# Q of two pieces moved from SyncE's queue to GpSimd's, a first GEMM in two column halves, earlier scaling of V, and a last quarter copied by two engines

## The chip, the cores and the metric

The kernel runs on 1 core of a Trainium2 chip (trn2). The metric is the time of one execution on the device in microseconds; the median of several runs is compared.

## The reference

The kernel computes a retention layer followed by a feed-forward block. There are 8 batches, 8 heads, 576 positions and a head size of 64; the feed-forward block has a width of 512 and an inner width of 2048.

```python
scores = scale * np.matmul(q, k.transpose(0, 1, 3, 2))
Dmat = np.where(rel >= 0, gamma[:, None, None] ** rel[None, :, :], 0.0)
x = np.matmul(scores * Dmat[None], v)          # (B, H, S, D)
x = x.transpose(0, 2, 1, 3).reshape(B * S, H * D)
h = x @ w_in
out = (h * np.clip(h + 3.0, 0.0, 6.0) / 6.0) @ w_out   # (4608, 512)
```

## The kernel before

The sequence of each batch is cut into four pieces of 128 positions and a rest of 64; the rests of two batches make one piece. There are 36 pieces, numbered c. For each piece Q, K and V are brought in for all heads ("thirds" of a piece, 128 rows of 8 x 64 numbers). The decay is folded into factors per position: Q and V are scaled, a mask leaves the lower triangle, and a state (K times V) is carried from piece to piece. `scale_v(c)` scales V on VectorE (L245), `k_by_pe` transposes K on TensorE and copies the result with ScalarE (L256, L257), `q_by_pe` does the same for Q through a product with a diagonal matrix (L265, L272), `scores` multiplies them and masks on VectorE (L347), `state_early` (L314 to L323) updates the state of pieces 0 to 3, `inter` and `intra` add up the piece's output (L361, L372), which ScalarE copies into `xt`, the transposed input of the first GEMM.

Tokens go through the feed-forward block in 9 blocks `kb` of 512 columns (four pieces each, the last block the rests). The first GEMM makes 16 row groups `fc` of 128 (`g1`, matmuls at L577, or `g1_columns` at L600 for a part of the columns), followed by an activation on ScalarE (L585) and a product on VectorE (L586). The second GEMM of blocks 0 and 1 goes over `w_out` directly (L635); from block 2 on it is made of seven products of half size (`g2_seven`, L720), whose results are added or copied and stored by quarter. In the last block the last quarter is copied in two halves by `copy_half` (L751), each followed by its own stores (L625); the other quarters are stored by `store_quarter` (L688), one half by SyncE's (SP's) queue and one by ScalarE's.

The order of instructions on each engine is the order in which the program is written (a manual schedule); each engine takes its own in order and waits on semaphores. The functions `first_step`, `step_first` and `step_second` place the work of later pieces between the units of the GEMMs.

Transfers: GpSimd's queue brings K and V (and Q from piece 4 on) and the weights, with a cast from float32 to float16 on the way (L103, L131, L136). Q of pieces 0 to 3 comes by SP's queue as float32 (`load_q`, L120), those of 2 and 3 held until a matmul of piece 0 has been issued, and is cast by ScalarE (`cast_q`, L128). The first GEMM of block 0 begins with `g1_first`: the first two row groups over all 512 columns, in two halves of the inner dimension.

Of the kernel before, what the change touches and what calls it, by code (L numbers as in the profile page):

```python
# [17 lines left out]
def kernel(  # L18
# [16 lines left out]
    nc = tc.nc  # L35
# [3 lines left out]
    P = 128  # L39
# [4 lines left out]
    MBLK = 512  # L44
# [48 lines left out]
    NBUF = 11  # L93

    def load_third(c, i):
        if i == 0:
            kn = nat.tile([P, H, D], FP16, tag="kn", bufs=NBUF, name=f"kn_{c}")
            qv = nat.tile([P, 2, H, D], FP16, tag="qv", bufs=NBUF, name=f"qv_{c}")
            loaded[c] = {"kn": kn, "qv": qv, "q16": qv[:, 0], "dma": []}
        dst, src = ((loaded[c]["kn"], k), (loaded[c]["qv"][:, 0], q),  # L100
                    (loaded[c]["qv"][:, 1], v))[i]
        for p0, b, s0, n in pieces[c][3]:
            loaded[c]["dma"].append(nc.gpsimd.dma_start(  # L103
                dst[p0:p0 + n], src[b, :, s0:s0 + n, :].rearrange("h s d -> s h d")))

    def load(c):
        for i in range(3):
            load_third(c, i)

    def load_kv(c):  # L110
        load_third(c, 0)
        load_third(c, 2)

    plain_q = {}

    def load_q(c, after=None):
        qf = work.tile([P, H, D], FP32, tag="osb", bufs=4, name=f"qf_{c}")
        plain_q[c] = qf
        (p0, b, s0, n), = pieces[c][3]
        moved = nc.sync.dma_start(qf, q[b, :, s0:s0 + n, :].rearrange("h s d -> s h d"))  # L120
        if after is not None:
            tc.add_manual_dep(
                moved.ins, after.ins.name,
                mybir.DependencyInfo(mybir.DependencyClass.Sync, mybir.DependencyReason.DATA),
                reason="the first pieces have the queues")

    def cast_q(c):
        nc.scalar.copy(loaded[c]["q16"], plain_q[c])  # L128
# [16 lines left out]
    load_q(0)  # L145
    load_q(1)
    load_kv(0)
    zeros = const.tile([P, MBLK], FP16)
    nc.vector.memset(zeros, 0.0)
    cb = const.tile([P, 2], FP32)  # L150
# [446 lines left out]
    def g1_columns(kb, fc, ph, cols):  # L597

        for dmc in range(NCC):
            nc.tensor.matmul(ph[:, cols], win16[:, dmc, P * fc:P * fc + P],  # L600
                             xt_of(kb)[:, dmc, cols],
                             start=(cols.start == 0 and dmc == 0),
                             stop=(cols.stop == MBLK and dmc == NCC - 1),
                             skip_group_check=True)
        if cols.stop == MBLK:
            g1_act(kb, ph, fc)

    def g1_first(kb):

        banks = [g1_bank(kb, fc) for fc in range(2)]  # L610
        for dmcs in ((0, 1), (2, 3)):
            for fc in range(2):
                g1_mm(kb, banks[fc], fc, dmcs)
        for fc in range(2):
            g1_act(kb, banks[fc], fc)

    def store(kb, mc, cols, src):
        if kb < B:
# [59 lines left out]
    def store_quarter(kb, i, j, src):  # L678

        cols = slice(NH * j, NH * j + NH)  # L680
        if kb < B:
            r0 = kb * S + TH * i
            nc.sync.dma_start(out[r0:r0 + TH, cols].rearrange("(u p) n -> p u n", u=2), src)
        else:
            rest = out.rearrange("(m x s) n -> x s m n", x=2, s=S)
            for x in range(2):
                queue = nc.scalar if x else nc.sync
                queue.dma_start(rest[x, MAIN:S, 2 * i:2 * i + 2, cols],  # L688
                                src[x * HALF:x * HALF + HALF])

    def g2_seven(kb, last=False):

        gt = gts[kb]

        def w(i, j):
            return wout16[:, KH * i:KH * i + KH, NH * j:NH * j + NH]

        def a(i, j):
            return gt[:, KH * j:KH * j + KH, TH * i:TH * i + TH]

        def s(name):
            return sums[kb, name]

        acc = {}

        def get(name):
            if name not in acc:
                if last and name == "x":
                    acc[name] = [psum.tile([P, NH], FP32, tag=t, name=f"x{t}_{kb}")
                                 for t in ("o", "tu")]  # L710
                else:
                    whole = bank([P, 2, NH], FP32, name=f"{name}_{kb}")
                    acc[name] = [whole[:, 0], whole[:, 1]]
                    wholes[name] = whole
            return acc[name]

        def product(name, u, left, right, first):
            dst = get(name)[u]
            for c in range(KH):
                newest[0] = nc.tensor.matmul(  # L720
                    dst, left()[:, c, P * u:P * u + P], right[:, c, :],
                    start=(first and c == 0 and (u == 0 or name not in wholes)),
                    stop=(c == KH - 1), skip_group_check=True)

        kept, wholes = {}, {}

        def parts(name, tile):
            if name in wholes:
                return [(wholes[name], tile)]
            return [(acc[name][u], tile[:, u]) for u in range(2)]  # L730

        def keep(name):
            kept[name] = work.tile([P, 2, NH], FP32, tag="keep_" + {"m5": "m1"}.get(name, name), bufs=1,
                                   name=f"keep_{name}_{kb}")
            for src, dst in parts({"m5": "z"}.get(name, "x"), kept[name]):
                nc.scalar.copy(dst, src)

        def total(i, j, name, src):
            osb = work.tile([P, 2, NH], FP32, tag="osb", bufs=4, name=f"osb_{kb}_{i}_{j}")
            for (a0, dst), (_, a1) in zip(parts(src, osb), parts(src, kept[name])):  # L740
                nc.vector.tensor_tensor(out=dst, in0=a0, in1=a1, op=ALU.add)
            store_quarter(kb, i, j, osb)

        def copy_total():
            osb = work.tile([P, 2, NH], FP32, tag="osb", bufs=4, name=f"osb_{kb}_1_0")
            nc.scalar.copy(osb, wholes["x"])
            store_quarter(kb, 1, 0, osb)

        def copy_half(u):
            osb = work.tile([P, NH], FP32, tag="osb", bufs=4, name=f"osh_{kb}_{u}")  # L750
            nc.scalar.copy(osb, acc["x"][u])  # L751
            store(kb, 2 + u, slice(0, NH), osb)

        def unit(name, u, left, right, first, then=()):
            def do():
                product(name, u, left, right, first)
                for f in then:
                    f()
            return do

        plan = [
            ("x", lambda: a(0, 0), w(0, 0), True, [lambda: keep("m1")]),
            ("y", lambda: a(0, 1), w(1, 0), True,
             [lambda: total(0, 0, "m1", "y"), lambda: token_sums(kb, "s3")]),
            ("x", lambda: s("s2"), wts["t2"], False, [lambda: keep("u2")]),
            ("z", lambda: s("s1"), wts["t1"], True,
             [lambda: keep("m5"), lambda: token_sums(kb, "s4")]),
            ("x", lambda: s("s3"), wts["t3"], False, [lambda: total(1, 1, "m5", "x")]),
            ("z", lambda: s("s4"), w(1, 1), False, [lambda: total(0, 1, "u2", "z")]),
            ("x", lambda: a(1, 1), wts["t4"], False, [] if last else [copy_total]),  # L770
        ]
        units = []
        for n, (name, left, right, first, then) in enumerate(plan):
            for u in range(2):
                after = then if u else []
                if last and n == len(plan) - 1:
                    after = [lambda u=u: copy_half(u)]
                units.append(unit(name, u, left, right, first, after))
        return units
# [1 line left out]


    WQ = DFF // 4
    for c in range(1, EARLY):
        load_kv(c)
    load_win(0, WQ // 2)
    load_win(WQ // 2, WQ)
    for i in range(1, 4):
# [5 lines left out]

    scale_v(0)
    q_by_pe(0)
    load_q(2, newest[0])
    warm(2, MBLK)
    cast_q(1)
    k_by_pe(0)  # L800
    load_q(3, newest[0])
    fill_gfull()
    for c in range(EARLY):
        if c:
# [2 lines left out]
        if c < EARLY - 1:  # L807
            scores(c)
            run_later(9)
            if c:  # L810
                k_by_pe(c + 1)
            state_early(c)
            run_later(9)
            if not c:
                k_by_pe(c + 1)
            q_by_pe(c + 1)
            if c + 2 < EARLY:
                cast_q(c + 2)
            scale_v(c + 1)
        else:  # L820
            scores_last(c)
# [40 lines left out]
    def first_step(c):  # L862


        old, new, b = c - 1 >= EARLY, c + 1 < 8, pieces[c - 1][1]
        if old:
            before = state_of.get(b)
            o = bank_or(None if c == 6 else "o", [P, NPAIR, P], FP32, name=f"o_{c - 1}")
# [20 lines left out]
            copy()  # L889
        if c < 8:  # L890
            run_later(9)
        if EARLY <= c < 8:
            scale_v(c)

    def transpose_q_and_load(c):

# [205 lines left out]
```

## Time and profile before

| | us |
|---|---|
| median of 3 runs | 294.66 (294.29 to 294.87) |
| the profiled execution, its own time | 294.43 |
| its span in the profile | 292.6 |
| TensorE busy | 281.1 |
| VectorE busy | 227.6 |
| ScalarE busy | 169.1 |
| GpSimd busy | 104.3 |

The granted TensorE clock was 1.0 of full speed throughout. In a line of the timeline the first number is the start, the second the time taken, both in us from the start of the span; then follow the engine (PE is TensorE, PEld its weight load, DVE VectorE, ACT ScalarE, POOL GpSimd, SP SyncE; a q behind the name is the engine's queue of transfers), the line of the kernel, the operation with its output and inputs, and in brackets the idle time of the engine before it and what ended that. A line of the chain of waits has a start, a duration and what took it. A line of the windows has the stretch, its length and the busy time of TensorE, its weight loads, VectorE, ScalarE and GpSimd. A line of the issues of transfers has the size and the median time from the issue to the landing.

### The profile page before, as it was taken

The page shows a single profiled execution, that of the slowest core. Times are in us where ns is not written, and L with a number is a line of the kernel's source. Part 1 is how long each engine was busy: PE and PEld are TensorE (multiplying, and loading weights), DVE is VectorE, ACT ScalarE, POOL GpSimd, SP SyncE. Part 2 cuts the span into 40 slices and gives each one's busy share as a digit, 9 for nine tenths or more (in the row PEclk, how much of TensorE's full clock was granted, in tenths as well). Part 3 has the DMA queues.
Part 4 walks back from the last instruction along what each step waited for, and adds up shares of the span by engine and source line. Part 5 has one row for each costly group of instructions (what it writes and reads, how often), then busy time and mean ns, then how long its engine had stood idle before and what let it go on. Part 6 is the DMA issues. An engine that isn't in the chain of part 4 may idle for free.

```text
span 292.6 us, 8351 instructions
## 1 busy us (share of the span) xinstructions
PE 281.1 (96%) x3492; PEld 174.7 (60%) x3492; DVE 227.6 (78%) x377; ACT 169.1 (58%) x301; POOL 104.3 (36%) x130
## 2 busy tenths in 40 slices
PE   7699999999989999999999999999999999999993
PEld 2454445544544587458745874587458745874682
DVE  4858656798758997899789988998899588728860
ACT  6668537784357744774486448644864286338711
POOL 8753578159523432443234324455550000000000
PEclk9999999999999999999999999999999999999999
DMA  9999999999999989997999799979992240120014
GB/s 137 177 205 203 191 157 215 165 126 137 132 215 166 160 85 120 168 141 81 121 163 143 77 127 170 136 82 123 160 139 47 74 110 0 38 81 30 0 39 109
DMA packets 156631, 36.21 MB, mean 124 GB/s; under 512 B 143792, under 2 KB 155568, under 8 KB 156592
## 3 DMA queue, kind: packets, MB, share of 16 engines
q0 software_dynamic: 113104, 17.83, 89.3%
q1 hardware_dynamic: 42896, 17.31, 30.5%
q8 instruction: 27, 0.44, 0.7%
q10 hardware_dynamic: 592, 0.52, 0.5%
q14 instruction: 12, 0.10, 0.1%
HBM read 36.70 MB, written 9.44 MB: 158 GB/s over the span
## 4 chain that ended last, share of the span: by engine, by line
PE 91%; DMA 4%; POOL 2%; DVE 1%; issue 1%; ACT 0%; ACTq 0%; POOLq 0%
PE ph L577 41%; PE x L720 14%; PE pout L635 9%; PE z L720 8%; PE y L720 5%; DMA kn<-in_k_dram 3%; PE o L483 3%; PE sc L450 2%; PE o L504 1%; PE u L535 1%; PE ph L600 1%; POOL kn L103 1%; DMA out_dram<-osb 1%; PE xtu L720 1%; PE xo L720 1%
## 5 line engine op out<-in xcount | busy, mean ns | idle before, releaser
L577 PE MATMUL ph<-xt,win 128*128 128x512 f16 x560 | 122.3, 379 | 0.0
L586 DVE SCALAR_TENSOR_TENSOR gt<-u,ph 128x512 f16<-128x512 f32 x144 | 95.7, 685 | 22.6 <-ACT u L585 21.4
L585 ACT ACTIVATE u<-ph,cb 128x512 f32<-128x512 f32 x144 | 98.4, 688 | 25.7 <-PE ph L577 25.1
L577 PEld LDWEIGHTS <-win 128*128 128x128 f16 x560 | 54.7, 98 | 64.4
L103 POOL DMA_DIRECT2D kn<-in_k_dram x40 | 34.0, 850 | 40.7 <-PE ph L577 15.4
L103 POOL DMA_DIRECT2D qv<-in_v_dram x40 | 33.8, 846 | 38.8 <-PE ph L577 16.2
L720 PEld LDWEIGHTS <-sum_s 128*128 128x128 f16 x448 | 42.7, 98 | 5.3
L103 POOL DMA_DIRECT2D qv<-in_q_dram x36 | 30.2, 839 | 28.7 <-PE z L720 10.4
L720 PEld LDWEIGHTS <-gt 128*128 128x128 f16 x336 | 32.1, 98 | 5.5
L635 PE MATMUL pout<-wout,gt 128*128 128x512 f16 x128 | 29.6, 379 | 0.1
L720 PE MATMUL x<-wsum_t,sum_s 128*128 128x256 f16 x192 | 22.9, 273 | 0.0
L556 ACT CAST tm<-th 128x256 f16<-128x256 f32 x24 | 9.7, 405 | 20.3 <-DVE th L551 20.1
L635 PEld LDWEIGHTS <-gt 128*128 128x128 f16 x128 | 11.9, 98 | 13.2 <-issue 0.4
L456 DVE TENSOR_TENSOR at<-sc,mask 128x1024 f16<-128x1024 f32 x14 | 17.0, 1217 | 1.9 <-PE sc L450 1.9
L676 DVE TENSOR_TENSOR sum_s<-gt 128x1024 f16<-128x1024 f16 (+1 forms) x21 | 18.1, 864 | 0.2
L332 DVE TENSOR_TENSOR qv<-qv,gqv 128x1024 f16<-128x1024 f16 x26 | 17.8, 684 | 0.0
L514 ACT CAST xt<-o 128x512 f16<-128x512 f32 x28 | 15.0, 585 | 4.6 <-PE o L504 4.6
L567 DVE TENSOR_TENSOR ta<-u,th 128x256 f32<-128x256 f32 x24 | 10.2, 424 | 6.3 <-ACT th L554 5.2
L720 PE MATMUL z<-wout,sum_s 128*128 128x256 f16 x112 | 14.5, 274 | 0.0
L720 PE MATMUL y<-wout,gt 128*128 128x256 f16 x112 | 14.3, 273 | 0.0
L720 PE MATMUL z<-wsum_t,sum_s 128*128 128x256 f16 x112 | 13.6, 273 | 0.0
L720 PE MATMUL x<-wout,gt 128*128 128x256 f16 x96 | 11.5, 272 | 0.0
(118 smaller groups left out, 255.3 us busy)
## 6 DMA issues: line engine op xcount, KB each, us to landing
out_dram<-osb SPq DMA_DIRECT2D x32, 256.0 KB, 3.2
kn<-in_k_dram POOLq DMA_DIRECT2D x32, 128.0 KB, 5.9
qv<-in_v_dram POOLq DMA_DIRECT2D x32, 128.0 KB, 6.0
qv<-in_q_dram POOLq DMA_DIRECT2D x28, 128.0 KB, 5.9
wout<-in_moe_w_out_dram POOLq DMA_DIRECT2D x4, 512.0 KB, 15.2
win<-in_moe_w_in_dram POOLq DMA_DIRECT2D x3, 512.0 KB, 12.3
qf<-in_q_dram SPq DMA_DIRECT2D x4, 256.0 KB, 4.6
win<-in_moe_w_in_dram POOLq DMA_DIRECT2D x2, 256.0 KB, 8.3
```

Of the source, the lines that this page charges most:

```text
L103: loaded[c]["dma"].append(nc.gpsimd.dma_start(dst[p0:p0 + n], src[b, :, s0:s0 + n, :].rearrange("h s d -> s h d")))
L332: scaled = nc.vector.tensor_tensor(out=qv, in0=qv, in1=gqv, op=ALU.mult)
L456: nc.vector.tensor_tensor(out=at.rearrange("t a j p s -> t (a j p) s"), in0=sc.rearrange("t a j p s -> t (a j p) s"), in1=mask64[:, None, ...
L514: nc.scalar.copy(xt_at(cs[0], 0, 2 * P).rearrange("e p (j x s) -> e p j x s", j=2, x=2) [:, :, :, half, :], o[half].rearrange("e j p s -> ...
L556: nc.scalar.copy(tm, ta)
L567: nc.vector.tensor_tensor(out=ta, in0=st[c]["u"][1], in1=st[c]["sum"], op=ALU.add)
L577: newest[0] = nc.tensor.matmul(ph, win16[:, dmc, P * fc:P * fc + P], xt_of(kb)[:, dmc, :], start=(dmc == 0), stop=(dmc == NCC - 1))
L585: nc.scalar.activation(u, ph, ACTF.Relu, bias=cb[:, 0:1], scale=1.0 / 6.0)
L586: nc.vector.scalar_tensor_tensor(out=gts[kb][:, fc, :], in0=u, scalar=1.0, in1=ph, op0=ALU.min, op1=ALU.mult)
L635: nc.tensor.matmul(pout, gt[:, fc, P * mc:P * mc + P], wout16[:, fc, :], start=(fc == 0), stop=(fc == NFC - 1))
L676: nc.vector.tensor_tensor(out=s(which)[:, c0:c1], in0=x(), in1=y(), op=op)
L720: newest[0] = nc.tensor.matmul(dst, left()[:, c, P * u:P * u + P], right[:, c, :], start=(first and c == 0 and (u == 0 or name not in whol ...
```

## The change

Six edits. (1) `load_q` is used for pieces 0 and 1 only; Q of pieces 2 and 3 comes by GpSimd's queue, already cast, ahead of K and V of the same piece (`load_qkv`); K and V of piece 1 keep their place behind those of piece 0. (2) In the loop over the first pieces Q's product comes ahead of K's transposition for every piece, and both after the state product. (3) `g1_first` makes the first two row groups in two halves of 256 columns each, over the whole inner dimension. (4) `first_step` scales V of pieces 4 to 7 at its beginning and not at its end. (5) In the last block, one half of the quarter of the first rows and second columns is stored by GpSimd's queue in place of ScalarE's. (6) In the last block, the second half of the last quarter is copied by VectorE in place of ScalarE.

```diff
--- before.py
+++ after.py
@@ -93,7 +93,7 @@
     NBUF = 11
 
     def load_third(c, i):
-        if i == 0:
+        if c not in loaded:
             kn = nat.tile([P, H, D], FP16, tag="kn", bufs=NBUF, name=f"kn_{c}")
             qv = nat.tile([P, 2, H, D], FP16, tag="qv", bufs=NBUF, name=f"qv_{c}")
             loaded[c] = {"kn": kn, "qv": qv, "q16": qv[:, 0], "dma": []}
@@ -107,22 +107,21 @@
         for i in range(3):
             load_third(c, i)
 
+    def load_qkv(c):
+        for i in (1, 0, 2):
+            load_third(c, i)
+
     def load_kv(c):
         load_third(c, 0)
         load_third(c, 2)
 
     plain_q = {}
 
-    def load_q(c, after=None):
+    def load_q(c):
         qf = work.tile([P, H, D], FP32, tag="osb", bufs=4, name=f"qf_{c}")
         plain_q[c] = qf
         (p0, b, s0, n), = pieces[c][3]
-        moved = nc.sync.dma_start(qf, q[b, :, s0:s0 + n, :].rearrange("h s d -> s h d"))
-        if after is not None:
-            tc.add_manual_dep(
-                moved.ins, after.ins.name,
-                mybir.DependencyInfo(mybir.DependencyClass.Sync, mybir.DependencyReason.DATA),
-                reason="the first pieces have the queues")
+        nc.sync.dma_start(qf, q[b, :, s0:s0 + n, :].rearrange("h s d -> s h d"))
 
     def cast_q(c):
         nc.scalar.copy(loaded[c]["q16"], plain_q[c])
@@ -145,6 +144,7 @@
     load_q(0)
     load_q(1)
     load_kv(0)
+    load_kv(1)
     zeros = const.tile([P, MBLK], FP16)
     nc.vector.memset(zeros, 0.0)
     cb = const.tile([P, 2], FP32)
@@ -597,7 +597,7 @@
     def g1_columns(kb, fc, ph, cols):
 
         for dmc in range(NCC):
-            nc.tensor.matmul(ph[:, cols], win16[:, dmc, P * fc:P * fc + P],
+            newest[0] = nc.tensor.matmul(ph[:, cols], win16[:, dmc, P * fc:P * fc + P],
                              xt_of(kb)[:, dmc, cols],
                              start=(cols.start == 0 and dmc == 0),
                              stop=(cols.stop == MBLK and dmc == NCC - 1),
@@ -608,11 +608,9 @@
     def g1_first(kb):
 
         banks = [g1_bank(kb, fc) for fc in range(2)]
-        for dmcs in ((0, 1), (2, 3)):
+        for cols in (slice(0, MBLK // 2), slice(MBLK // 2, MBLK)):
             for fc in range(2):
-                g1_mm(kb, banks[fc], fc, dmcs)
-        for fc in range(2):
-            g1_act(kb, banks[fc], fc)
+                g1_columns(kb, fc, banks[fc], cols)
 
     def store(kb, mc, cols, src):
         if kb < B:
@@ -684,7 +682,7 @@
         else:
             rest = out.rearrange("(m x s) n -> x s m n", x=2, s=S)
             for x in range(2):
-                queue = nc.scalar if x else nc.sync
+                queue = (nc.gpsimd if j > i else nc.scalar) if x else nc.sync
                 queue.dma_start(rest[x, MAIN:S, 2 * i:2 * i + 2, cols],
                                 src[x * HALF:x * HALF + HALF])
 
@@ -748,7 +746,10 @@
 
         def copy_half(u):
             osb = work.tile([P, NH], FP32, tag="osb", bufs=4, name=f"osh_{kb}_{u}")
-            nc.scalar.copy(osb, acc["x"][u])
+            if u:
+                nc.vector.tensor_copy(osb, acc["x"][u])
+            else:
+                nc.scalar.copy(osb, acc["x"][u])
             store(kb, 2 + u, slice(0, NH), osb)
 
         def unit(name, u, left, right, first, then=()):
@@ -781,8 +782,8 @@
 
 
     WQ = DFF // 4
-    for c in range(1, EARLY):
-        load_kv(c)
+    for c in range(2, EARLY):
+        load_qkv(c)
     load_win(0, WQ // 2)
     load_win(WQ // 2, WQ)
     for i in range(1, 4):
@@ -794,11 +795,9 @@
 
     scale_v(0)
     q_by_pe(0)
-    load_q(2, newest[0])
     warm(2, MBLK)
     cast_q(1)
     k_by_pe(0)
-    load_q(3, newest[0])
     fill_gfull()
     for c in range(EARLY):
         if c:
@@ -807,15 +806,10 @@
         if c < EARLY - 1:
             scores(c)
             run_later(9)
-            if c:
-                k_by_pe(c + 1)
             state_early(c)
             run_later(9)
-            if not c:
-                k_by_pe(c + 1)
             q_by_pe(c + 1)
-            if c + 2 < EARLY:
-                cast_q(c + 2)
+            k_by_pe(c + 1)
             scale_v(c + 1)
         else:
             scores_last(c)
@@ -863,6 +857,8 @@
 
 
         old, new, b = c - 1 >= EARLY, c + 1 < 8, pieces[c - 1][1]
+        if EARLY <= c < 8:
+            scale_v(c)
         if old:
             before = state_of.get(b)
             o = bank_or(None if c == 6 else "o", [P, NPAIR, P], FP32, name=f"o_{c - 1}")
@@ -889,8 +885,6 @@
             copy()
         if c < 8:
             run_later(9)
-        if EARLY <= c < 8:
-            scale_v(c)
 
     def transpose_q_and_load(c):
```

## The prediction

> **What bounds the kernel now.** I read the page, then the chain that ended last (its start and its end), TensorE's waits, and the timeline of the places that the diff touches.
>
> ```profile
> span 292.6 us, 8351 instructions
> PE 281.1 (96%) x3492; PEld 174.7 (60%) x3492; DVE 227.6 (78%) x377; ACT 169.1 (58%) x301; POOL 104.3 (36%) x130
> ```
> ```profile
> 0.00:18.20 18.20, 13.14 (x153) 7.17 (x154) 11.87 (x37) 12.05 (x26) 14.60 (x22) 1.00 1.56 166
> ```
> ```profile
> PE trk L256 <- DMA kn<-in_k_dram: 2.2, 2, 1.2
> ...
> PE o L504 <- issue: 0.9, 1, 0.9
> ...
> PE o L372 <- DVE qv L245: 0.5, 1, 0.5
> ```
>
> TensorE is busy for 281.1 of 292.6 us. Of the 11.5 us that are not, 5.1 lie in the first 18.20 us (the windows row: 13.14 busy). So time can be won in three places only: before the first GEMM, in the few waits after it, and behind the last matmul. The waits name two that the diff touches, K (2.2 us) and the scaling of V at L245 (0.5 us). The 0.9 us at L504 has no releaser; nothing in the diff reaches it, and I count it as staying.
>
> ```profile
> 6.75 7.55 DMA kn<-in_k_dram
> ...
> 14.34 0.40 PE trk L256 x4
> ...
> 15.52 0.33 PE o L361 x4
> 15.85 0.34 PE o L372 x8
> 16.20 0.37 PE sc L283 x8
> ...
> 18.23 3.77 PE ph L577 x17
> ```
>
> The chain says what the first GEMM waits for: K of piece 3, issued by GpSimd at 6.75, lands 7.55 us later at 14.30, and everything from there to 18.23 is work behind that landing (3.89 us after the transposition's start).
>
> **Part 1: where Q of pieces 2 and 3 is loaded.** Landings are read from what waited for them.
>
> ```profile
> 6.16 0.22 PEld L256 LDWEIGHTS <-kn 128*128 128x128 f16 x4 [0.81 <-DMA kn<-in_k_dram]
> ...
> 6.75 0.93 POOL L103 DMA_DIRECT2D kn<-in_k_dram  x1
> ...
> 7.11 0.42 DVE L245 TENSOR_TENSOR qv<-qv,gqv 128x512 f16<-128x512 f16 x1 [1.88 <-DMA qv<-in_v_dram]
> ...
> 7.96 0.23 PEld L256 LDWEIGHTS <-kn 128*128 128x128 f16 x4 [0.16 <-DMA kn<-in_k_dram]
> ...
> 8.48 3.79 POOL L131 DMA_DIRECT2D win<-in_moe_w_in_dram  x5
> ...
> 10.51 0.62 ACT L128 CAST qv<-qf 128x512 f16<-128x512 f32 x1 [1.05 <-DMA qf<-in_q_dram]
> ...
> 11.09 0.40 PE L256 MATMUL trk<-ident,kn 128*128 128x128 f16 x4 [1.17 <-DMA kn<-in_k_dram]
> ```
>
> K0, V0 and K1 land at 6.16, 7.11 and 7.96: 0.90 us each. Then the pace breaks: K1 at 7.96, K2 at 11.09, K3 at 14.30, 6.34 us for four transfers of GpSimd's queue (V1, K2, V2, K3), 1.59 each. In that stretch SP's Q of pieces 2 and 3 went through as well; the ACT row shows Q2 landing at 10.51. Counted as six transfers it is 1.06 each.
>
> After the change the same six go through one queue: Q2, K2, V2, Q3, K3 follow V1. If each takes the 0.90 us that this queue shows when it runs alone, K3 lands at 7.96 + 6 x 0.90 = 13.4. If the six cost 1.06 each, it lands at 14.3, as now. I take 13.4: the 0.90 rows are the same queue, source and shape, and no transfer of SP's is left between the early Q0 and Q1 and the first store. GpSimd's issues keep up: from 6.75 to 8.48 two of them take 1.73 us, 0.87 each, so K3's issue moves by two, to 8.48, 4.9 us ahead of 13.4.
>
> ```profile
> DMA to landing us min/median/max: 4.5/4.6/4.6
> ```
>
> That is more than the 4.6 us from issue to landing of K1 and V1 (the answer for GpSimd's loads in the stretch 4:5), so the issue does not hold it.
>
> The Trainium skill speaks against this move: Perfetto Trace Analysis, DMA Optimizations, advises to spread transfers over the engines that can issue them when descriptor generation is the limit, and here two transfers move onto the one queue that is full of issues (GpSimd's 14.60 of 18.20 us). By that rule K3 comes later; it is the third rival.
>
> **Part 2: the order behind K3.** Now K3's transposition is followed on TensorE by the state product, Q's product and the outputs of piece 2 before the scores at 16.20: 1.86 us after 14.34. In the changed order state and Q come ahead of K (Q lands first), so behind K3 lie its transposition (0.40) and the two output products (0.33 and 0.34): 1.07 us.
>
> ```profile
> 14.78 0.59 ACT L257 COPY qk<-trk 128x512 f16<-128x512 f16 x1 [0.28 <-PE trk L256]
> ```
>
> The scores also need ScalarE's copy of K: 0.44 us after the transposition's start, then 0.59: 1.03 us. Both ways the scores start about 1.07 after the landing, 0.79 sooner. I take 0.7, since that copy now queues behind Q's. The two casts (0.62 us each) leave ScalarE, which gains nothing more by itself. Sum of parts 1 and 2: 0.9 + 0.7 = 1.6 us, first GEMM at about 16.6. Ends: 0.7 (K3 at 14.3) and 1.75.
>
> The 256-column start costs nothing and brings nothing here: the chain shows no wait between the last output product and 18.23, TensorE takes its instructions in order, and 16 matmuls of half the width replace 8.
>
> Two covers have to hold for the 1.6 us to last.
>
> ```profile
> 20.71 0.75 POOL L136 DMA_DIRECT2D wout<-in_moe_w_out_dram  x1 [1.48 <-DMA win<-in_moe_w_in_dram]
> ```
> ```profile
> 28.29 0.88 POOL L103 DMA_DIRECT2D qv<-in_q_dram  x1 [1.24 <-DMA wout<-in_moe_w_out_dram]
> DMA to landing us min/median/max: 11.8/11.8/11.8
> ```
> ```profile
> 41.39 0.41 PE L265 MATMUL trq<-dq,qv 128*64 128x128 f16 x8
> ```
>
> First, the second 512 columns of w_in: this GpSimd row was released when they landed, 20.7. They are wanted 16 matmuls into the GEMM (17 take 3.77 us, so 3.5): now at 21.7, then at 20.1. The queue behind V3 moves up with K3, to 19.8, so 0.3 us of cover is left; if it did not move, 0.6 us would be lost. Second, Q of piece 5: 28.29 + 11.8 = 40.1, wanted at 41.39; then 39.2 against 39.8. Later loads are released by instructions of this kernel that move along.
>
> **Part 3: V of pieces 4 to 7.**
>
> ```profile
> 48.58 1.22 DVE L347 TENSOR_TENSOR at<-sc,mask_wide 128x1024 f16<-128x1024 f32 x1
> ...
> 49.72 0.41 DVE L245 TENSOR_TENSOR qv<-qv,gqv 128x512 f16<-128x512 f16 x1
> ...
> 50.19 0.41 PE L372 MATMUL o<-at,qv 128*64 128x128 f16 x8 [0.47 <-DVE qv L245]
> ```
>
> TensorE idles 0.47 us because VectorE scales V after the mask. Put ahead of the step, the 0.41 us fall into VectorE's idle time before the state update, and the outputs wait for the mask alone, ready at 49.72: 0.4 us gained, between 0 and 0.47. If V had not landed, the update and the mask queued behind the scaling would wait; in this trace each scaling ran right behind its mask, with no wait for a transfer, and it moves up by less than 3 us. The other three scalings did not stop TensorE.
>
> **Part 4: the last quarter.**
>
> ```profile
> 284.25 0.42 DVE L741 TENSOR_TENSOR osb<-xtu,keep_m 128x256 f32<-128x256 f32 x1 [0.39 <-PE xtu L720]
> ...
> 286.00 0.69 DVE L741 TENSOR_TENSOR osb<-z,keep_u 128x512 f32<-128x512 f32 x1 [1.32 <-PE z L720]
> 286.67 1.04 PE L720 MATMUL xtu<-wsum_t,gt 128*128 128x256 f16 x8
> 287.45 0.37 ACT L751 COPY osh<-xo 128x256 f32<-128x256 f32 x1 [4.30 <-DMA out_dram<-osb]
> ...
> 288.49 0.37 ACT L751 COPY osh<-xtu 128x256 f32<-128x256 f32 x1 [0.66 <-ACT osh L751]
> 288.89 0.51 ACTq L625 DMA_DIRECT2D out_dram<-osh  x1
> ```
> ```profile
> kn<-in_k_dram POOLq DMA_DIRECT2D x32, 128.0 KB, 5.9
> ...
> kn<-in_k_dram POOLq DMA_DIRECT2D x8, 64.0 KB, 3.8
> ...
> out_dram<-osh ACTq DMA_DIRECT2D x2, 64.0 KB, 2.3
> ```
>
> The last matmuls end at 287.71, but ScalarE copies their half only at 288.49, after a store issue, the other copy and another issue. VectorE is free from 286.69: its copy starts at about 287.75, takes the 0.42 of the row with the same shape, and the last stores start at 288.2 instead of 288.89: 0.7 us. They land 2.3 later, 290.5 against 291.2. In exchange a 128 KB store leaves GpSimd's queue at 286.7; the nearest row, half-height loads on that queue, takes 3.8 to landing, so 290.5; the 4.6 of the start gives 291.3. I take 0.6, between -0.1 and 0.7. The Trainium skill (DMA: Bandwidth & Descriptors, Anatomy of one DMA) estimates 2.0 us plus the bytes over 436 GB/s for such a transfer, 2.3 us here; by it the store hides and the term is 0.7.
>
> **Sum.** 1.6 + 0.4 + 0.6 = 2.6 us. The profiled execution took 294.43 (span 292.6, 1.8 around it, untouched), the median 294.66, 0.2 more; 294.66 - 2.6 = 292.1.
>
> **Rivals.**
> *The queue is no faster alone.* The six transfers still take 1.06 each: K3 at 14.3, terms 0.7 + 0.4 + 0.6 = 1.7, so 292.9. For it: the engines' bytes are the same. Against: the 0.90 rows. 0.18.
> *Slower: GpSimd's queue has a pace of 1.59 of its own.* Then Q2 and Q3 push K3 to 7.96 + 6 x 1.59 = 17.5, the GEMM starts at 17.5 + 3.2 = 20.7, 2.4 later than now; less 1.0 from the other parts, 296.1. It decides from K3 at 16.0 on (14.3 + 0.7 + 1.0), 1.35 per transfer. For it: that pace held from 7.96 to 14.30. Against: it began when SP's Q came. 0.09.
> *The issue decides.* K3 lands 7.55 after its issue as now: 8.48 + 7.55 = 16.0, nothing is left: 294.6. This is what the Trainium skill's rule cited in part 1 would do. Against it: the 4.6 us rows. 0.04.
> *GpSimd's store ends the kernel.* At the 5.9 us that a 128 KB load takes at the median over the whole span, 292.6, 1.4 later than the last store now: 2.0 - 1.4 = 0.6 gained, 294.1. Against: the queue is empty by then. 0.03.
>
> **How the numbers follow.** The forecast 292.1 has 0.66; its own range, from the ends of the terms and the 0.9 us without a releaser coming or going, is 291.1 to 292.9. With the first rival the range is 291.0 to 293.4. A measurement of this kernel can tell about 0.2% (0.6 us). Faster: 0.66 + 0.18 = 0.84; same: 0.04 + 0.03 = 0.07; slower: 0.09.
>
> **What would show it.** In the changed profile K2 and K3 land about 10.8 and 13.4, the scores of piece 3 start about 1.1 us later, the first L577 or L600 matmul of block 0 at 16.6; no wait of TensorE for L245; VectorE's copy of the last half at about 2.2 us before its landing, and no store of GpSimd's after that. Wrong would be K3 beyond 14.3, a wait for w_in inside the first GEMM, for Q of piece 5 or 6 behind it, or a GpSimd store that lands last.

## Result and the profile after

| | before | after |
|---|---|---|
| median of 21 runs each, taken side by side | 294.87 us | 292.63 us |
| lowest to highest | 293.02 to 296.57 | 291.24 to 295.36 |
| the profiled execution, its own time | 294.43 us | 291.25 us |
| its span | 292.6 us | 289.5 us |

The ratio is 0.9928 with a 95% interval of 0.9908 to 0.9947, so the changed kernel is faster by about 2.1 us (1.6 to 2.7). Ratios here and below are taken over the fast executions of each kernel, nearly all of them, and a size in us that stands with a ratio is worked out from it, so it can differ from the difference of the two medians. The prediction was 292.1 us, 2.6 us faster, with a range of 291.0 to 293.4.

First the page of the changed kernel. Span and busy times show that TensorE works as long as before (281.3 us against 281.1) and that its idle time has shrunk from 11.5 to 8.2 us.

```profile
span 289.5 us, 8362 instructions
...
PE 281.3 (97%) x3500; PEld 175.2 (61%) x3500; DVE 227.7 (79%) x378; ACT 167.4 (58%) x298; POOL 106.7 (37%) x133
```

TensorE's waits of the changed kernel (what it waited for, us in total, times, longest):

```profile
PE sc L343 <- ACT qk L257: 1.0, 2, 0.7
PE sc L283 <- ACT qk L257: 0.3, 1, 0.3
PE o L372 <- DVE at L347: 0.3, 1, 0.3
PE ph L577 <- DMA win<-in_moe_w_in_dram: 0.2, 1, 0.2
PE trq L265 <- DMA qv<-in_q_dram: 0.2, 1, 0.2
...
PE u L314 <- DVE qv L245: 0.2, 1, 0.2
```

The 2.2 us for K, the 0.5 us for the scaled V at L372 and the 0.9 us of L504 are gone. In their place stand two short waits for transfers, w_in inside the first GEMM and Q of piece 5 behind it: the two covers that the prediction had left at 0.3 and 0.6 us. A wait of 0.2 us for a scaled V is left, at the state product of piece 3 (L314). The 0.3 us of L372 for the mask (L347) is not new: it stands at 9.05, in the first pieces, and the kernel before has it at 8.96.

The timeline at the start, from the issue of K of piece 3 to the second GEMM:

```profile
8.49 0.94 POOL L103 DMA_DIRECT2D kn<-in_k_dram  x1
...
13.33 0.40 PE L256 MATMUL trk<-ident,kn 128*128 128x128 f16 x4
...
14.63 0.40 PE L283 MATMUL sc<-qk 64*128 64x128 f16 x8 [0.34 <-ACT qk L257]
...
16.76 0.61 PE L600 MATMUL ph<-xt,win 128*128 128x256 f16 x4
...
20.63 10.53 PE L577 MATMUL ph<-xt,win 128*128 128x512 f16 x48 [0.23 <-DMA win<-in_moe_w_in_dram]
31.00 1.24 PE L633 MATMUL pout<-wout,gt 128*128 128x512 f16 x5
```
```profile
DMA to landing us min/median/max: 4.7/4.7/4.8
```

The second fence is the answer for the two loads of GpSimd issued at 7.62 and 8.49, Q and K of piece 3: 4.7 us after its issue K is there, at 13.2, and is transposed at once. The scores of piece 3 follow 1.3 us after the start of that transposition and the first GEMM begins at 16.76. In the timeline of the kernel before, the second GEMM began here:

```profile
31.99 1.24 PE L635 MATMUL pout<-wout,gt 128*128 128x512 f16 x5
```

So 0.99 us of the start reached the second GEMM in this execution. The timeline at the end:

```profile
284.31 1.04 PE L718 MATMUL xtu<-wsum_t,gt 128*128 128x256 f16 x8
284.51 0.37 ACT L752 COPY osh<-xo 128x256 f32<-128x256 f32 x1 [3.73 <-PE xo L718]
284.62 0.62 POOL L686 DMA_DIRECT2D out_dram<-osb  x1 [69.40 <-DVE osb L739]
284.91 1.43 ACTq L623 DMA_DIRECT2D out_dram<-osh  x2
285.04 1.33 SPq L623 DMA_DIRECT2D out_dram<-osh  x2
285.38 0.42 DVE L750 COPY osh<-xtu 128x256 f32<-128x256 f32 x1 [1.05 <-PE xtu L718]
```
```profile
out_dram<-osb POOLq DMA_DIRECT2D x1, 128.0 KB, 2.7
out_dram<-osh ACTq DMA_DIRECT2D x2, 64.0 KB, 2.5
out_dram<-osh SPq DMA_DIRECT2D x2, 64.0 KB, 2.6
```

VectorE copies the last half right behind its matmuls. GpSimd's store, issued at 284.62, lands 2.7 us later (the second fence, transfers issued from 284 us on), 287.3, ahead of the last stores. From the start of the last matmul group to the end of the span it was 5.9 us (286.67 to 292.6) and is 5.2 (284.31 to 289.5): 0.7 us less.

The 3.1 us between the two spans are made up thus. The scores of pieces 10 and 11 (L450) begin at 74.68 before and 73.64 after: 1.04 us. The 0.47 us of the scaled V are in that, so of the 1.41 us by which the first GEMM began sooner (18.17 to 16.76) about 0.6 were still there. The stall of 0.94 us at L504 comes behind them and is missing after, with 0.38 us of small gaps around it. The tail brings 0.7. The medians differ by 2.1 to 2.2 us only, because the profiled execution of after, with 291.25, is one of the quickest of its 21 runs, while that of before lies 0.4 under its median: a profile shows where time went in one execution, and the medians say how much of it is there every time.

### The profile page after: what moved, and what is told of

It is laid out like the page before. It is cut to its first block, busy times and chain, and to the rows that moved or that the text cites. A ratio compares the mean times of both kernels' runs of the same rounds, so it can differ in the third digit from the quotient of the medians.

```text
span 289.5 us, 8362 instructions
## 1 busy us (share of the span) xinstructions
PE 281.3 (97%) x3500; PEld 175.2 (61%) x3500; DVE 227.7 (79%) x378; ACT 167.4 (58%) x298; POOL 106.7 (37%) x133
## 4 chain that ended last, share of the span: by engine, by line
PE 84%; DMA 9%; POOL 4%; DVE 1%; issue 0%; POOLq 0%
PE ph L577 37%; PE x L718 14%; PE z L718 9%; PE pout L633 6%; DMA wout<-in_moe_w_out_dram 5%; PE y L718 5%; DMA qv<-in_q_dram 4%; PE o L483 3%; POOL qv L103 2%; PE sc L450 2%; PE o L504 1%; PE u L535 1%; POOL kn L103 1%; PE ph L600 1%; POOL win L130 1%; PE xtu L718 1%
## 5 line engine op out<-in xcount | busy, mean ns | idle before, releaser
L577 PE MATMUL ph<-xt,win 128*128 128x512 f16 x552 | 120.8, 379 | 0.2 <-DMA win<-in_moe_w_in_dram 0.2
L577 PEld LDWEIGHTS <-win 128*128 128x128 f16 x552 | 53.9, 98 | 64.0 <-DMA win<-in_moe_w_in_dram 0.7
L718 PEld LDWEIGHTS <-sum_s 128*128 128x128 f16 x448 | 42.7, 98 | 5.3
L103 POOL DMA_DIRECT2D qv<-in_q_dram x38 | 32.1, 846 | 29.7 <-PE z L718 8.0
L718 PEld LDWEIGHTS <-gt 128*128 128x128 f16 x336 | 32.0, 98 | 5.5
L686 POOL DMA_DIRECT2D out_dram<-osb x1 | 0.6, 620 | 69.4 <-DVE osb L739 69.4
L718 PE MATMUL x<-wsum_t,sum_s 128*128 128x256 f16 x192 | 22.9, 273 | 0.0
L718 PE MATMUL z<-wout,sum_s 128*128 128x256 f16 x112 | 14.5, 274 | 0.0
L718 PE MATMUL y<-wout,gt 128*128 128x256 f16 x112 | 14.3, 273 | 0.0
L718 PE MATMUL z<-wsum_t,sum_s 128*128 128x256 f16 x112 | 13.6, 273 | 0.0
```

The lines of the kernel that those rows point to most:

```text
L103: loaded[c]["dma"].append(nc.gpsimd.dma_start(dst[p0:p0 + n], src[b, :, s0:s0 + n, :].rearrange("h s d -> s h d")))
L577: newest[0] = nc.tensor.matmul(ph, win16[:, dmc, P * fc:P * fc + P], xt_of(kb)[:, dmc, :], start=(dmc == 0), stop=(dmc == NCC - 1))
L718: newest[0] = nc.tensor.matmul(dst, left()[:, c, P * u:P * u + P], right[:, c, :], start=(first and c == 0 and (u == 0 or name not in whol ...
```

## The experiments

Each kernel was timed beside the kernel before on the same chip, and the median of that stands with each. One profile was taken of each kernel.

**Which part brings what.** The kernel before with one part of the change at a time. First the loads and their order (edits 1 and 2):

```diff
+    load_kv(1)
...
-    for c in range(1, EARLY):
-        load_kv(c)
+    for c in range(2, EARLY):
+        load_qkv(c)
...
-    load_q(2, newest[0])
...
-    load_q(3, newest[0])
...
-            if c:
-                k_by_pe(c + 1)
             state_early(c)
...
             q_by_pe(c + 1)
-            if c + 2 < EARLY:
-                cast_q(c + 2)
+            k_by_pe(c + 1)
             scale_v(c + 1)
```

> The kernel before with Q of pieces 2 and 3 on GpSimd's queue and Q ahead of K, nothing else. Theory: the first GEMM starts about 1.4 us sooner (16.75), but the pieces of w_in and Q of piece 5 land no sooner than before, so three waits (w_in twice, Q of piece 5 once) give about 0.6 back: 0.8 us faster than before. Rival (the cover held, as the prediction had it): 1.6 us faster and no such waits. Second rival (the column halves are needed for the early start): under 0.5 us, with the first GEMM at 17 or later.

293.79 us against 294.28, ratio 0.9971 (0.9945 to 0.9997): 0.85 us faster. The size is the one expected; the three waits that were to explain it are not there. In its timeline the whole 1.6 us of the forecast are there, at the first GEMM (16.57) and still at the second (30.40 against 31.99), and no transfer of w_in was waited for:

```profile
16.57 1.25 PE L577 MATMUL ph<-xt,win 128*128 128x512 f16 x5
...
30.40 0.81 PE L635 MATMUL pout<-wout,gt 128*128 128x512 f16 x3
...
64.68 1.28 SPq L333 DMA_TRANSPOSE qk<-qv  x1
...
73.09 0.32 PE L450 MATMUL sc<-qk 64*64 64x64 f16 x16
74.24 0.32 PE L450 MATMUL sc<-qk 64*64 64x64 f16 x16 [0.83 <-DMA qk<-qv]
```
```profile
DMA to landing us min/median/max: 9.5/9.5/9.5
```

The time is lost at 74 us: the scores of piece 11 wait 0.83 us for its transposed Q, which SP's queue issued at 64.68 and which took 9.5 us to land (the second fence, for this one transfer). In the kernel before the same transfer and the same scores read:

```profile
65.70 1.20 SPq L333 DMA_TRANSPOSE qk<-qv  x1
...
74.68 0.45 PE L450 MATMUL sc<-qk 64*64 64x64 f16 x32
```
```profile
DMA to landing us min/median/max: 7.5/7.5/7.5
```

There it landed at 73.2, with 1.5 us to spare. So with TensorE 1.6 us ahead, the transposition was issued only 1.0 us sooner, and it landed 1.0 us later than before. The 0.6 us at the issue are lost in SP's queue: an earlier transposition took it 2.22 us to issue (at 58.33; 1.51 us before, at 59.93), and the next four issues follow behind it without a gap of more than 0.1 us. But this loss does not by itself explain the 0.85: the profiled execution took 292.26, 2.2 us less than the profiled one of before (the stall at L504 is missing in it) and 1.5 us less than the median of its own kernel. Where the usual execution loses time no profile shows, and the interval, 0.1 to 1.6 us, just reaches the 1.6 of the start.

Then the scaling of V alone (edit 4):

```diff
         old, new, b = c - 1 >= EARLY, c + 1 < 8, pieces[c - 1][1]
+        if EARLY <= c < 8:
+            scale_v(c)
...
-        if EARLY <= c < 8:
-            scale_v(c)
```

> The kernel before with only the scaling of V of pieces 4 to 7 at the beginning of the step. Theory: TensorE's wait of 0.47 us on L245 goes and nothing takes its place: 0.4 us faster. Rival (the time is given back later, at the next wait for a mask or a transfer): no difference.

293.67 against 294.28, 0.9982 (0.9959 to 1.0004): 0.5 us at the middle, and not told from nothing by the times alone. TensorE's waits in its profile have no L245 at L372 any more; the loads, the start and the tail wait as before.

Then the last quarter alone (edits 5 and 6):

```diff
-                queue = nc.scalar if x else nc.sync
+                queue = (nc.gpsimd if j > i else nc.scalar) if x else nc.sync
...
-            nc.scalar.copy(osb, acc["x"][u])
+            if u:
+                nc.vector.tensor_copy(osb, acc["x"][u])
+            else:
+                nc.scalar.copy(osb, acc["x"][u])
```

> The kernel before with only the two edits of the last block. Theory: the last stores start 0.7 us sooner, GpSimd's store lands before them: 0.7 us faster. Rival (GpSimd's store lands last): 0.1 us faster or slower.

293.74 against 294.28, 0.9976 (0.9954 to 0.9999): 0.7 us. In its timeline VectorE's copy follows the last matmul group as in the changed kernel:

```profile
285.83 1.04 PE L720 MATMUL xtu<-wsum_t,gt 128*128 128x256 f16 x8
...
286.90 0.43 DVE L752 COPY osh<-xtu 128x256 f32<-128x256 f32 x1 [1.06 <-PE xtu L720]
```

From the last group's start to the span's end (291.3) it is 5.5 us, against 5.9 before. The three middles add up to 0.85 + 0.5 + 0.7 = 2.1 us, the middle of the whole change. Each has an interval of 0.6 to 0.8 us either way, so the sum alone does not show that nothing is left for the column halves.

**The order without the loads.** The kernel before, with Q's product ahead of K's transposition only:

```diff
-            if c:
-                k_by_pe(c + 1)
             state_early(c)
             run_later(9)
-            if not c:
-                k_by_pe(c + 1)
             q_by_pe(c + 1)
             if c + 2 < EARLY:
                 cast_q(c + 2)
+            k_by_pe(c + 1)
             scale_v(c + 1)
```

> The kernel before with Q's product ahead of K's transposition alone; Q of pieces 2 and 3 still comes by SyncE's queue and is cast by ScalarE. Theory: K of piece 3 lands at 14.3 as before, the scores start 1.1 after it, the first GEMM at about 17.5, and w_in is there in time: 0.7 us faster, nearly all that the loads and the order bring together. Rival (the order helps only because Q lands ahead of K): the cast holds Q's product, 0.3 us faster or less.

296.24 against 294.28, 1.0052 (1.0027 to 1.0078): slower by 1.5 us, where 0.7 faster was expected. TensorE's waits and ScalarE's and TensorE's timelines say where:

```profile
PE sc L343 <- ACT qk L257: 1.9, 3, 1.1
```
```profile
10.11 0.62 ACT L128 CAST qv<-qf 128x512 f16<-128x512 f32 x1 [0.40 <-DMA qf<-in_q_dram]
10.63 0.58 ACT L257 COPY qk<-trk 128x512 f16<-128x512 f16 x1
...
11.27 0.61 PE L343 MATMUL sc<-qk 64*128 64x128 f16 x8 [1.08 <-ACT qk L257]
```

ScalarE takes its instructions in order, and the cast of the Q that SP brings now stands ahead of the copy of K. It waits for that Q to land, the copy behind it waits too, and TensorE waits for the copy. The first GEMM began at 20.49. The held copy is not all of that: the waits for it grew by 1.2 us (1.9 against 0.7 before), and TensorE ran at about half speed up to 17 us in this profile. The same transposition of four matmuls took 0.61 us at 13.34 and 0.40 at 17.17:

```profile
13.34 0.61 PE L256 MATMUL trk<-ident,kn 128*128 128x128 f16 x4
...
17.17 0.40 PE L256 MATMUL trk<-ident,kn 128*128 128x128 f16 x4
```

With the cast behind the copy this wait should go (the edit is to the kernel just told):

```diff
             q_by_pe(c + 1)
+            k_by_pe(c + 1)
             if c + 2 < EARLY:
                 cast_q(c + 2)
-            k_by_pe(c + 1)
             scale_v(c + 1)
```

> The kernel before with Q's product ahead of K's transposition, as in the run order_only, but with ScalarE's cast of the next Q behind the copy of K. Theory (order_only was slow because the cast, waiting for SyncE's Q, held the copy of K): no wait of over 0.4 us of the scores for that copy, the first GEMM at 17.2 to 17.6, 0.3 to 0.7 us faster than before. Rival (Q by SyncE lands too late for this order, wherever the cast stands): no faster than before, with the first GEMM at 18 or later.

294.23 against 294.37, 0.9992 (0.9975 to 1.0009): the loss is gone, so the place of the cast was its cause. The waits are as the theory said (for the copy of K of pieces 1 to 3 none is over 0.34 us), but no gain appears. The interval, 0.3 us slower to 0.7 us faster, holds both the expected gain and none. The first GEMM began at 18.64 in its profile, as the rival had it, but not for the rival's reason: TensorE waited for no Q there after piece 0, and it ran at half speed from about 8 to 14 us. So these times show no gain of the order while Q comes by SP's queue, and whether there is one at full speed stays open. And with the loads moved, is the order worth something? The changed kernel with K's transposition ahead again:

```diff
+            if c:
+                k_by_pe(c + 1)
             state_early(c)
             run_later(9)
+            if not c:
+                k_by_pe(c + 1)
             q_by_pe(c + 1)
-            k_by_pe(c + 1)
             scale_v(c + 1)
```

> The changed kernel with K's transposition ahead of the state product and of Q's product again. If the order is worth 0.7 us where K lands last, the first GEMM starts at about 17.3 and the kernel is up to 0.7 us slower than the changed one; but a start at 17.3 meets no wait for w_in, so by the theory that those waits take the early start back only 0.2 to 0.4 us are lost. Without that theory: 0.7.

292.87 against 294.82, 0.9916 (0.9885 to 0.9947), in 6 runs: not told from the changed kernel's 0.9928. With an interval of 0.9 us either way the 0.7 us of the order are neither confirmed nor refuted. Its profile can't settle it, since TensorE ran at half speed there for some microseconds (below) and the first GEMM began at 18.29. The wait for the transposed Q of piece 11 is there as well: 0.51 us.

**The column halves.** The changed kernel with the first two row groups in halves of the inner dimension, as before:

```diff
-        for cols in (slice(0, MBLK // 2), slice(MBLK // 2, MBLK)):
+        for dmcs in ((0, 1), (2, 3)):
             for fc in range(2):
-                g1_columns(kb, fc, banks[fc], cols)
+                g1_mm(kb, banks[fc], fc, dmcs)
+        for fc in range(2):
+            g1_act(kb, banks[fc], fc)
```

> The changed kernel with the first two row groups of the first GEMM in two halves of the inner dimension again. Theory: no difference (within 0.2 us), since the start waits for w_in and for the order on TensorE. Rival (the halves let the GEMM start before the last copies): 0.3 us or more slower than the changed kernel, with a wait of TensorE for the copy at L306.

292.21 against 294.82, 0.9920 (0.9887 to 0.9952), with the first GEMM at 16.61 and no wait ahead of it for w_in or for the copies: edit 3 is worth nothing that the times can tell. In this profile (span 289.2) the second GEMM began at 30.44, so the full 1.55 us of the start were there, and the transposed Q of piece 11 took 7.6 us and was not waited for.

**What holds the first weights.** The changed kernel without the load of Q of piece 3:

```diff
-        for i in (1, 0, 2):
+        for i in ((1, 0, 2) if c < 3 else (0, 2)):
             load_third(c, i)
+        if c == 3:
+            loaded[c]["q16"] = loaded[2]["q16"]
```

> The changed kernel without the load of Q of piece 3 (piece 2's Q is used in its place). If w_in's landing is set by all that is queued ahead of it, one transfer less brings w_in and Q of piece 5 about 1.0 us sooner, the three waits vanish and the kernel is 0.6 to 1.1 us faster than the changed one. If w_in lands by a pace of its own whatever is ahead, it still lands at about 16.7, 18.7 and 20.8 and the waits stay.

292.14 against 294.82, 0.9898 (0.9865 to 0.9931), in 4 executions: 0.9 us below the changed kernel by the middles, but the intervals overlap. In its profile the waits for w_in and for Q of piece 5 are gone, which says little, since TensorE ran at half speed up to 13 us there and the first GEMM began only at 18.82. GpSimd's first issue for w_out that is released by the second 512 columns of w_in reads, in this kernel, in loads_order, and in the changed one:

```profile
19.60 0.76 POOL L137 DMA_DIRECT2D wout<-in_moe_w_out_dram  x1 [2.25 <-DMA win<-in_moe_w_in_dram]
```
```profile
20.10 0.75 POOL L135 DMA_DIRECT2D wout<-in_moe_w_out_dram  x1 [1.34 <-DMA win<-in_moe_w_in_dram]
```
```profile
20.88 0.75 POOL L135 DMA_DIRECT2D wout<-in_moe_w_out_dram  x1 [1.27 <-DMA win<-in_moe_w_in_dram]
```

With one third of a piece less in the queue w_in lands 0.5 to 1.3 us sooner, which speaks for a landing that hangs on what is queued ahead of it, on a single profile. Before it was 20.71, and with the loads moved 20.09 to 20.16 in four profiles, 0.6 sooner; the profiled execution of the changed kernel is the exception, and its waits for w_in (0.20 on a weight load at 16.75, and 0.23) and for Q of piece 5 (0.21) go with that. Would smaller transfers help? The second 512 columns in two:

```diff
-    for i in range(1, 4):
+    load_win(WQ, WQ + WQ // 2)
+    load_win(WQ + WQ // 2, 2 * WQ)
+    for i in range(2, 4):
         load_win(i * WQ, i * WQ + WQ)
```

> The changed kernel with the second 512 columns of w_in in two transfers of 256. Theory: the row groups that are wanted first land about 1.2 us sooner, the wait of 0.23 us at the ninth row of the first GEMM goes, 0.2 us faster than the changed kernel. Rival (one more issue on GpSimd's queue shifts the later loads): Q of piece 5 comes later by as much, no difference.

292.98 against 294.82, 0.9933 (0.9898 to 0.9967): no gain. In its profile the first 256 columns of w_in came late instead, with 0.83 us of waiting ahead of the first GEMM (at 17.40), and the transposed Q of piece 11 took 8.7 us.

**The early clock.** In four of the twelve profiles TensorE's work ahead of the first GEMM runs at half speed beyond the first 7 us: order_only up to 17 us, no_q3 up to 13, order_cast_last and old_order from about 8 to 14. These are the four with the latest first GEMM (20.49, 18.82, 18.64, 18.29; the changed kernel 16.76). The windows of the one that ran old_order (stretch, its length, busy time of TensorE, its weight loads, VectorE, ScalarE, GpSimd; then the granted clock, 0.50 from 8 to 14 us):

```profile
6.00:8.00 2.00, 1.01 (x16) 0.74 (x16) 0.60 (x2) 1.49 (x4) 2.00 (x3) 0.94 2.30 146
8.00:14.00 6.00, 5.58 (x64) 3.90 (x64) 4.23 (x6) 2.91 (x7) 6.00 (x9) 0.50 2.59 155
14.00:18.00 4.00, 3.74 (x58) 2.49 (x55) 3.44 (x5) 2.54 (x6) 3.23 (x4) 0.93 1.33 202
```

In that stretch the transposition of K, four matmuls, takes 0.61 us in place of 0.40, and the product of Q, eight matmuls, 0.64 in place of 0.41. In order_only and no_q3 the same durations stand beside a clock column of 1.00, and the mean clock of both is listed as 0.998, so the listed clock does not show every such stretch. The Trainium skill (TensorE: Matmul & The Clock Gate, Part 1: The HAM clock gate) says that the unit runs at half rate by default, that a free-running window of about 3.4 us of activity decides, and that the number of slow matmuls changes from run to run; the 0.50 and its coming in some profiles agree. If the half speed sets the spread of the times, filler matmuls at the start should narrow it:

```diff
     k_by_pe(0)
+    warm(2, 384)
     fill_gfull()
```

> The changed kernel with two more matmuls on zeros (384 columns) in the gap of 0.7 us between K's transposition and the scores of piece 0. Theory (whether TensorE runs at full speed in the first 17 us depends on how much it works around 3 to 8 us, and differs from execution to execution): the slow executions become rarer, the mean granted clock rises, the median falls by 0.3 to 0.8 us against the changed kernel, its fastest executions stay as they are. Rival (the differences between executions come from the transfers): median unchanged.

292.78 against 294.37, 0.9955 (0.9921 to 0.9988). The mean granted clock was never below 0.992, where 6 of the 21 executions of the changed kernel had 0.986 to 0.988, but the times were no better: 290.88 and 293.76 us both came at a listed clock of 1.0. Since that clock can miss half-speed stretches, this does not show how much of the spread the clock makes; that stays open. No kernel tried is clearly quicker than the changed one.

## Why the prediction was right, point by point

**Sign and size.** 2.6 us were forecast and 2.1 measured, inside the range. Three terms were named, and each of the one-part kernels has a gain at the middle, that of the scaling alone not told from nothing by its times. The start's term was too large (1.6 against 0.85 at the middle), and a part of the measured gain may come from the stall at L504, which no term had, so it is partly luck that the sum came within 0.5 us.

**Loads on one queue: right in its mechanism.** K of piece 3 was to land at 13.4 and the first GEMM to begin at 16.6; they came at 13.2 and 16.76 (16.57 and 16.61 in the profiles of loads_order and no_columns). The six transfers run at the pace of the 0.90 rows once SP's loads of Q of pieces 2 and 3 are out of the way, so the rivals "the queue is no faster alone" (14.3), "the issue decides" (16.0) and the pace of 1.59 (17.5) are all refuted by that one landing. What that pace is, the prediction read wrongly. It took the 0.90 us for the pace of a queue that runs alone, but SP's Q of piece 2 had been issued at 5.33, while K0, V0 and K1 were still on their way; and it said that the issue does not hold K3. In the changed kernel every transfer from K0 to K3 lands 4.5 to 4.8 us after its own issue, and the issues follow each other every 0.87 us, so the pace is that of GpSimd's issues. Before, K0, V0, K1 and V1 landed 4.5 to 4.8 us after theirs, and K2, V2 and K3, with SP's two loads under way, after 6.0, 7.0 and 7.5. The number came out because the two paces are nearly the same, 13.4 by the one and 8.49 + 4.7 = 13.2 by the other.

The Trainium skill advises to spread transfers over the engines that can issue them if descriptor generation is the limit (Perfetto Trace Analysis, DMA Optimizations). Before the change it was not the limit for K of piece 3, which landed 7.5 us after its issue, so the condition of the advice was not met there. Moving two transfers onto the fullest queue brought the last of them 1.1 us sooner.

**The step that failed** is the sentence "Later loads are released by instructions of this kernel that move along", with the two covers before it. The 1.6 us of the start were sized for the first GEMM and carried to the end unchanged; loads_order, which has them alone, brought 0.85 at the middle. Its profile shows 0.83 us given back at L450 and old_order 0.51: the transposed Q of piece 11 is issued sooner by less than TensorE is ahead, and lands later after its issue. In the five profiles with Q still on SP's queue it took 6.9 to 7.9 us to land; in loads_order 9.5, old_order 9.4, warm_fill 8.8, split_win 8.7, and 7.6, 7.1 and 6.7 in the others. (split_win waited 0.25 us at L450 too, but at 82.24, for a later piece.) In the profile of the changed kernel the loss was at the two covers instead (0.64 us in three waits). So w_in and Q of piece 5 were rightly named, but the sentence "The queue behind V3 moves up with K3" was mis-sized: w_in's second part was to land at 19.8, 0.9 us sooner, and landed 0.6 sooner in four profiles and 0.2 later in that of the changed kernel. Why the transposition takes longer was not tried. With an interval of 0.1 to 1.6 us for loads_order the size of the give-back rests on single profiles, and a share of the loss may be half-speed executions, which the prediction did not consider: no profile at full speed shows what the median execution loses.

**The order behind K3.** Inside the changed kernel the scores began 1.30 us after K's transposition, against 1.79 by the timeline of before (16.13 less 14.34; the chain's 1.86 counts from a later point), so 0.5 of the 0.7 are seen there. As a separate edit it shows no gain in the times (order_cast_last) or was not measurable (old_order), and in both profiles TensorE ran at half speed.

**The scaling of V.** The wait of 0.47 us is gone and 0.5 was measured for 0.4, with an interval that includes no gain. No wait has taken its place there: the outputs at 49.15 follow without one.

**The tail.** 0.6 forecast; 0.7 in the profile of the changed kernel, 0.5 in that of tail_only (5.93 to 5.47 us from the last group to the end) and 0.7 in its times. GpSimd's store landed in 2.7 us, not the 3.8 that the nearest row gave. The rival in which that store ends the kernel is refuted. The 2.3 us that the Trainium skill's formula gives (DMA: Bandwidth & Descriptors, Anatomy of one DMA) was closer to the measured 2.7.

**The column halves.** Nothing that the times can tell, as forecast.

**The stall at L504** was to stay. It did not, in the profile of the changed kernel (see the last section).

## What to carry to other kernels

When the first work of an engine moves forward, list everything that the later work waits for and ask of each whether it moves too: here the transfers of w_in and the transposed Q of piece 11 moved by less, and a gain at the start was in part paid back where one of them was late. An order that looks free can cost, since a cast that waits for a transfer holds all that is behind it on its engine. Compare the durations of equal instructions before putting a late start down to what it waits for: in four profiles here TensorE ran at half speed ahead of a late first GEMM. And when one execution's profile gives a larger gain than the medians, compare its own time with the spread of the runs before explaining the difference.

## What was not expected of the hardware

The stall of TensorE without a releaser sits at a fixed place: where it is at L504 it comes behind the tenth of 32 matmuls, as in the profiles of before and tail_only:

```profile
82.96 0.26 PE L504 MATMUL o<-at,qv 64*64 64x64 f16 x10
84.16 0.38 PE L504 MATMUL o<-at,qv 64*64 64x64 f16 x22 [0.94 <-issue]
```
```profile
82.46 0.26 PE L504 MATMUL o<-at,qv 64*64 64x64 f16 x10
83.30 0.37 PE L504 MATMUL o<-at,qv 64*64 64x64 f16 x22 [0.58 <-issue]
```

It is 0.5 to 0.9 us in the five profiles in which Q of pieces 2 and 3 comes by SP's queue, and in the seven with Q on GpSimd's it is missing (four) or 0.4 (three, two of them at L718). One profile of each kernel is little, and no run tests a cause; if the pattern holds, some 0.5 us of the gain comes from there (it would be inside the 0.85 of loads_order), which the prediction had in no term, only in the ends of its range.
